# One more down stage in seven block products, one batch's softmax numerators with their sums on ScalarE, and the column-max exchange moved to ScalarE

## The chip, the cores and the metric

The kernel runs on one core of one Trainium2 chip. A core has a matrix engine (PE, with its weight loads PEld), a vector engine (DVE), an activation engine (ACT), a general engine (POOL) and a queue engine for transfers (SP). Each engine takes its instructions strictly in the order of the program and waits at an instruction until the semaphores that it names have been reached. The metric is the device time of one launch in microseconds (us).

## The reference

Eight batches of a linear attention (8 heads, 576 tokens, 64 columns a head) feed one gated feed-forward block over all 4608 tokens:

```python
q_s = np.exp(q - np.max(q, axis=-1, keepdims=True)); q_s = q_s / (np.sum(q_s, axis=-1, keepdims=True) + 1e-09)
k_s = np.exp(k - np.max(k, axis=2, keepdims=True));  k_s = k_s / (np.sum(k_s, axis=2, keepdims=True) + 1e-09)
kv = np.einsum('bhsd,bhse->bhde', k_s, v)
x  = np.einsum('bhsd,bhde->bhse', q_s, kv)           # then (tokens, 512)
h  = (x @ w1) * (x @ w2) @ w3                         # 512 -> 1024 -> 1024
out = h @ w_out                                       # 1024 -> 512
```

q is normalised along a head's 64 columns, k along the 576 tokens. The kernel folds `w3 @ w_out` into one matrix `W3O` (1024 x 512) first.

## The kernel before, in words

**Tiles.** A batch's q, k and v lie in SBUF as 128 partitions: 64 rows of tokens x 2 halves of the heads, each with 4 heads x 9 token slots x 64 columns. The feed-forward works on nine groups of 512 tokens: groups 0 to 7 are the first 512 tokens of a batch each, group 8 gathers the 64 that remain of every batch (`xtail`).

**Steps of a batch b.** `qmx.b.p` (DVE) finds the row maxima of q, `qsub.b.p` (POOL or DVE) subtracts them, `qexp.b.p` (ACT) is the exponential, `qsm.b.p` (DVE) the row sum, `qeps.b.p`, `qrc.b.p` and `qn.b.p` add epsilon, invert and scale, and `qd.b.p` (a transposing transfer on SP's queue) turns the result. p is 0 (token slots 0 to 3, 1024 elements a partition) or 1 (slots 4 to 8, 1280 elements). For k, `kmi.b` (ACT) and `kmx.b` (DVE) find the column maxima within a partition, `cb.b` (eight DVE instructions: transpose, reduce, four small exchanges between neighbouring quarters of the partitions, reduce, transpose) spreads them over the partitions, `ksub.b.hp` subtracts, `kexp.b.hp` (ACT) is the exponential. `vc.b.hp` casts v. `kv.b` multiplies k and v (PE), `kv2.b` scales it, `xm.b` and `xt.b` multiply q with it (PE), and `xs.b`, `xts.b` copy the result x out of PSUM.

**Steps of a group c.** Up stage of groups 0 to 4: `up.1.c` and `up.0.c` (x @ w2, x @ w1; PE, tile `pab`), `bs.c` (copy one to SBUF), `ab.c` (DVE, their product). Up stage of groups 5 to 8: seven products of half-size blocks in place of eight, `um.c.g.1` to `um.c.g.7`, with the sums of blocks `xd`, `ws` before and the copies `ue` and combinations `uc`, `ab` behind. Down stage of groups 0 to 3 and 8: `down.c.t` (four blocks of 128 tokens, eight matmuls of 512 columns each, tile `po`), `os.c.t` copies it out, `st.c.t` stores it. Down stage of groups 4 to 7 (the list `SD`): seven products of half-size blocks, `dm.c.1` to `dm.c.7` (eight matmuls of 256 columns each, tiles `dA`, `dB`, `dC`), with the four block sums `ad.c.1` to `ad.c.4` before, and behind them the copies `de.c.1`, `.7`, `.2`, `.4` and the combinations `dc.c.1` to `dc.c.4`. Products 1, 6, 5 and 3 use one PSUM bank in turn: product 6 may begin only when `de.c.1` has copied product 1 out of it, product 5 only after `de.c.2`, product 3 only after `de.c.4`. The up stage has the same rule for `um.c.g.1`, `.6`, `.5`, `.3` with `ue.c.g.1`, `.2`, `.4`, and for `.7`, `.4` with `ue.c.g.7`.

**What sets the order.** The string `ORDER` lists every step once; a step's instructions are issued to its engine in that order, and a letter behind a slash (A, D, P) says which engine takes a step that several could take. What stands between two steps of different engines in the string has no effect but through PSUM banks and buffers. Steps that use the port that DVE and POOL share are linked, so that they follow each other as listed. PE's list begins with matmuls on zeros that lead nowhere (`zero`).

**The names that the change touches.** `SD` (L242), `FEXP` (L262), `cb` (L441), `qexps` (L537), `down` (L793), `dm` (L890), and `ORDER` (L83). `qexps` exists in the kernel before, and no batch uses it:

```python
for j in range(js.start, js.stop):
    x = hs.start + h
    nc.scalar.activation(out=st["eq", b, p][:, h, j - js.start, :], in_=qb[:, x, j, :],
                         func=AF.Exp, bias=st["qm", b][:, x, j:j + 1],
                         accum_out=st["qr", b][:, x, j:j + 1])
```

Of the kernel before, what the change touches and what calls it, by code (L numbers as in the profile page):

```python
# [93 lines left out]
qsub.1.0/P up.0.0.0.2 kexp.1.1 up.1.0.1.2 qmx.1.1 qsub.1.1/P qexp.1.0 ab.0.1.1 ab.0.0.2 qsm.1.0 qeps.1.0/D qrc.1.0  # L94
qn.1.0/P qd.1.0 kexp.1.0 k.3 up.0.0.0.3 ab.0.0.3 up.0.0.1.2 bs.0.1.2/A ab.0.1.2 qexp.1.1 vc.1.0/A qsm.1.1 qeps.1.1/A
ws.1.1/P ab.0.1.3 q.3 down.0.0 down.0.1 os.0.1/A down.0.2 qrc.1.1 qmx.2.0 kv.1.0 qn.1.1/P qmx.2.1 qsub.2.1/P vc.1.1/A
kv.1 kv2.1 os.0.0/A kmi.2 kmx.2.0 down.0.3 xm.1.0 xs.1.0.0/A xs.1.0.1/D up.1.1.0.0 up.0.1.0.0 kmx.2.1 os.0.2/A cb.2
qexp.2.1 qsm.2.1 bs.1.0.0/A qd.1.1 up.1.1.0.1 up.0.1.0.1 up.1.1.0.2 os.0.3/A bs.1.0.1/A qsub.2.0/P up.0.1.0.2
up.1.1.0.3 up.0.1.0.3 ws.2.1/P xm.1.1 v.2 ab.1.0.0 v.3 ab.1.0.1 xt.1 bs.1.0.2/A ab.1.0.2 qexp.2.0 qsm.2.0 bs.1.0.3/A
ksub.2.1/P ab.1.0.3 down.1.0 down.1.1 qeps.2.1/A qrc.2.1 ksub.2.0/P kmi.3 q.4 kmx.3.0 qeps.2.0/A qrc.2.0 xts.1.1/A  # L100
qmx.3.1 xs.1.1.0/A xs.1.1.1/A os.1.0/A up.1.1.1.0 up.0.1.1.0 up.1.1.1.1 kexp.2.1 qmx.3.0 up.0.1.1.1 qn.2.1/P
up.1.1.1.2 xts.1.0/A vc.2.1/A kmx.3.1 bs.1.1.0/A ab.1.1.0 cb.3 kexp.2.0 qd.2.1 vc.2.0/A bs.1.1.2/A up.0.1.1.2 ab.1.1.2
qn.2.0/P bs.1.1.1/A ab.1.1.1 os.1.1/A qsub.3.1/P qexp.3.1 kv.2 kv2.2 up.1.1.1.3 bs.1.1.3/D up.0.1.1.3 qd.2.0 ab.1.1.3
qsub.3.0/P qexp.3.0 qsm.3.0 ksub.3.0/P xm.2.1 xs.2.1.0/A xm.2.0 xs.2.0.1/A xt.2 xs.2.0.0/A ksub.3.1/P down.1.2 k.4
xs.2.1.1/A up.1.2.0.0 bs.2.0.0/A kexp.3.1 xts.2.1/A qsm.3.1 qeps.3.1/D xts.2.0/A kmi.4 up.0.2.0.0 up.1.2.0.1 st.0.3
up.0.2.0.1 qeps.3.0/A up.1.2.0.2 q.5 kexp.3.0 ws.3.0/D st.0.2 qrc.3.1 wt.1/D ab.2.0.0 bs.2.0.1/A up.0.2.0.2 qmx.4.1
bs.2.0.2/A up.1.2.0.3 vc.3.0/A up.0.2.0.3 qrc.3.0 qn.3.1/P qmx.4.0 up.1.2.0.4 os.1.2/A up.0.2.0.4 up.1.2.0.5 vc.3.1/A
bs.2.0.4/A kmx.4.0 qn.3.0/P ab.2.0.2 kmx.4.1 bs.2.0.5/A qmx.5.1 ab.2.0.1 bs.2.0.3/A ab.2.0.3 v.4 vc.4.1/A qsub.4.0/P
up.0.2.0.5 ab.2.0.4 qsub.4.1/P qexp.4.1 up.1.2.0.6 bs.2.0.6/A kv.3 kv2.3 st.0.1 qd.3.1 ab.2.0.5 qexp.4.0 ws.1.0/P
ws.2.0/D down.1.3 os.1.3/A qd.3.0 xm.3.0 st.0.0 xs.3.0.1/A xm.3.1 xs.3.1.1/A xt.3 xs.3.0.0/A qsub.5.1/P cb.4  # L110
ksub.4.0/P up.0.2.0.6 xts.3.0/A v.5 k.5 qsm.4.1 ab.2.0.6 up.1.2.0.7 xs.3.1.0/A q.6 up.0.2.0.7 up.1.3.0.0 vc.4.0/A v.6
bs.2.0.7/A qsm.4.0 qexp.5.1 bs.3.0.0/A qeps.4.0/A ab.2.0.7 up.0.3.0.0 up.1.3.0.1 up.0.3.0.1 up.1.3.0.2 up.0.3.0.2
st.1.1 qmx.5.0 bs.3.0.1/A ksub.4.1/P ab.3.0.1 qeps.4.1/A qrc.4.1 qrc.4.0 kmi.5 qn.4.0/P ab.3.0.0 up.1.3.0.3 up.0.3.0.3
kexp.4.0 kexp.4.1 k.6 bs.3.0.3/A kmx.5.0 up.1.3.0.4 bs.3.0.4/A qsm.5.1 qsub.5.0/P vc.5.1/A qexp.5.0 kmx.5.1 qeps.5.1/A
xts.3.1/D qn.4.1/P down.2.0 os.2.0/A ab.3.0.3 qmx.6.1 down.2.1 down.2.2 qsub.6.1/P os.2.1/A bs.3.0.2/A qmx.6.0
qsub.6.0/P cb.5 ksub.5.0/P kv.4 kv2.4 up.0.3.0.4 up.1.3.0.5 os.2.2/A qd.4.0 ab.3.0.2 up.0.3.0.5 up.1.3.0.6 up.0.3.0.6
bs.3.0.5/A ab.3.0.5 ksub.5.1/P kmi.6 qexp.6.1 qd.4.1 ab.3.0.4 xm.4.0 st.1.0 qsm.5.0 qrc.5.1 xm.4.1 down.2.3 xs.4.0.1/A
kmx.6.0 qexp.6.0 bs.3.0.6/A xs.4.0.0/D up.1.3.0.7 up.0.3.0.7 ab.3.0.6 xs.4.1.0/A xs.4.1.1/A up.1.4.0.0 up.0.4.0.0
up.1.4.0.1 st.2.2 ws.3.1/D q.7 qeps.5.0/A qrc.5.0 kexp.5.0 kmx.6.1 cb.6 qn.5.0/P qd.5.0 kexp.5.1 bs.4.0.0/A ab.4.0.0
bs.3.0.7/A qn.5.1/P ab.3.0.7 qsm.6.1 vc.6.1/A up.0.4.0.1 os.2.3/A st.2.3 bs.4.0.1/A up.1.4.0.2 up.0.4.0.2 vc.6.0/A  # L120
up.1.4.0.3 up.0.4.0.3 up.1.4.0.4 ab.4.0.1 bs.4.0.2/A ab.4.0.2 qd.5.1 st.1.3 vc.5.0/A qmx.7.0 kv.5 qsm.6.0 ksub.6.0/P
kexp.6.0 xt.4 xts.4.1/A up.0.4.0.4 qeps.6.1/A bs.4.0.4/A ab.4.0.4 kv2.5 bs.4.0.3/A ab.4.0.3 up.1.4.0.5 down.3.0
os.3.0/D st.1.2 up.0.4.0.5 xm.5.0 xm.5.1 ksub.6.1/P kexp.6.1 k.7 qeps.6.0/A qrc.6.0 qsub.7.0/P bs.4.0.5/A ab.4.0.5
wt.3/P qexp.7.0 qsm.7.0 xts.4.0/A kv.6 xs.5.0.1/A xt.5 xs.5.1.1/A xs.5.0.0/A xs.5.1.0/A up.1.4.0.6 qn.6.0/P bs.4.0.6/A
kv2.6 xd.5.3/P um.5.1.1 ue.5.1.1/A qmx.7.1 down.3.1 ws.4.0/D os.3.1/A xd.5.2/D um.5.0.7 ue.5.0.7/A ws.4.1/D xd.5.1/D
um.5.2.1 ue.5.2.1/A xts.5.1/A wt.2/D xts.5.0/A um.5.1.6 ue.5.1.2/A v.7 um.5.0.1 ue.5.0.1/A qeps.7.0/D um.5.1.7
xd.5.4/D kmi.7 wt.4/D down.3.2 qrc.6.1 qsub.7.1/P ue.5.1.7/A qd.6.0 um.5.0.6 um.5.1.4 ue.5.0.2/A kmx.7.0 qrc.7.0
uc.5.1.3 qn.6.1/P qd.6.1 um.5.1.5 ue.5.1.4/A uc.5.1.4/P qexp.7.1 kmx.7.1 um.5.0.4 vc.7.1/A um.5.0.5 uc.5.0.3 st.3.0
ue.5.0.4/A uc.5.0.4/P up.0.4.0.6 ab.4.0.6 um.5.3.1 um.5.2.6 qn.7.0/P up.1.4.0.7 bs.4.0.7/A um.5.2.7 qsm.7.1 um.5.1.3
ue.5.3.1/A cb.7 ksub.7.0/P down.3.3 os.3.2/A um.5.3.7 st.3.1 qeps.7.1/A ue.5.2.7/A um.5.2.4 ab.5.1.1 qrc.7.1 qn.7.1/P  # L130
ue.5.2.2/A uc.5.2.3 um.5.2.5 um.5.3.6 os.3.3/A um.5.1.2 uc.5.1.1 um.5.3.2 uc.5.3.1 um.5.0.3 ab.5.0.1 um.5.2.2 uc.5.2.1
ue.5.3.7/A um.5.3.4 ue.5.3.2/A uc.5.3.3 up.0.4.0.7 ab.4.0.7 vc.7.0/A um.5.3.5 ad.4.3/D ue.5.2.4/A ad.4.1/D um.5.2.3
xm.6.0 xm.6.1 xt.6 ue.5.3.4/A uc.5.3.4/D uc.5.2.4/D qd.7.0 um.5.3.3 xs.6.0.0/A xs.6.1.1/A xs.6.1.0/A dm.4.1 ad.4.2/D
xts.6.0/D dm.4.2 dm.4.7 xs.6.0.1/A um.6.2.1 ad.4.4/D de.4.1/A dm.4.6 xd.6.3/D ksub.7.1/D xts.6.1/D um.5.0.2 uc.5.0.1
kexp.7.0 de.4.7/A dm.4.4 st.3.2 de.4.2/A dm.4.5 dc.4.1 st.2.1 kexp.7.1 ab.5.2.0/P dc.4.3 ue.6.2.1/A um.6.2.7
ue.6.2.7/A de.4.4/A kv.7 qd.7.1 xd.6.2/D xd.6.4/D um.6.2.6 um.6.2.4 ab.5.2.1 dm.4.3 ue.6.2.2/A kv2.7 xd.6.1/P um.6.2.5
dc.4.2/A ab.5.3.0/P ab.5.3.1 ab.5.1.0/P xm.7.1 uc.6.2.3 xm.7.0 xt.7 xts.7.1/D ue.6.2.4/A uc.6.2.4/D xs.7.0.0/A
# [984 lines left out]
```

## Time and profile before

| what | us |
|---|---|
| median of three runs | 228.77 (228.55 to 229.41) |
| the profiled execution, its own time | 228.65 |
| its span, first to last instruction | 226.8 |
| PE busy in the span | 219.9 |
| DVE busy | 202.7 |
| ACT busy | 153.8 |
| POOL busy | 147.9 |

The profiled execution lies 0.12 us under the median, and 1.85 us of its time lie outside the span. In the profile a row of a group gives the line, the engine, the operation, the tiles (written <- read), the shapes, the count, the busy time and the mean length of one. PE's busy time is modelled: neighbouring matmuls overlap in it, so PE's pace is read from the starts of neighbouring groups or from the chain of work that ended last, which gives each piece the time until the next one. On ACT and DVE too an instruction's length is a little more than the distance to the next one.

### The profile page before, as it was taken

The page shows a single profiled execution, that of the slowest core. Times are in us where ns is not written, and L with a number is a line of the kernel's source. Part 1 is how long each engine was busy: PE and PEld are TensorE (multiplying, and loading weights), DVE is VectorE, ACT ScalarE, POOL GpSimd, SP SyncE. Part 2 cuts the span into 40 slices and gives each one's busy share as a digit, 9 for nine tenths or more (in the row PEclk, how much of TensorE's full clock was granted, in tenths as well). Part 3 has the DMA queues.
Part 4 walks back from the last instruction along what each step waited for, and adds up shares of the span by engine and source line. Part 5 has one row for each costly group of instructions (what it writes and reads, how often), then busy time and mean ns, then how long its engine had stood idle before and what let it go on. Part 6 is the DMA issues. An engine that isn't in the chain of part 4 may idle for free.

```text
span 226.8 us, 5607 instructions
## 1 busy us (share of the span) xinstructions
PE 219.9 (97%) x2226; PEld 148.2 (65%) x2226; DVE 202.7 (89%) x381; ACT 153.8 (68%) x250; POOL 147.9 (65%) x100
## 2 busy tenths in 40 slices
...
GB/s 223 212 274 248 298 223 248 372 376 268 342 386 267 286 410 233 264 395 390 168 181 199 152 343 124 98 188 158 3 132 56 0 95 92 3 92 3 95 185 185
DMA packets 38106, 46.89 MB, mean 207 GB/s; under 512 B 18112, under 2 KB 21568, under 8 KB 38080
## 3 DMA queue, kind: packets, MB, share of 16 engines
...
q8 instruction: 17, 0.28, 0.5%
q10 hardware_dynamic: 144, 0.07, 0.1%
q14 instruction: 9, 0.07, 0.1%
...
## 4 chain that ended last, share of the span: by engine, by line
PE 46%; DVE 25%; DMA 18%; ACT 3%; issue 3%; POOL 3%; SPq 1%; DVEq 0%; POOLq 0%
PE uA L858 12%; DMA q<-in_q_dram 7%; PE pab L774 6%; PE dA L899 6%; PE uB L858 6%; DVE ab L789 6%; DVE qm L521 5%; DMA v<-in_v_dram 5%; DMA w<-in_moe_w_dram 5%; DVE qr L553 4%; PE po L796 3%; PE uC L858 3%; PE dB L899 3%; PE po L811 3%; DVE kmp L433 2%
## 5 line engine op out<-in xcount | busy, mean ns | idle before, releaser
L774 PE MATMUL pab<-x,w2sb 128*128 128x256 f16 (+1 forms) x224 | 40.6, 318 | 0.8 <-ACT x L273 0.7
L774 PE MATMUL pab<-x,w1sb 128*128 128x256 f16 (+1 forms) x224 | 40.4, 318 | 0.0
L458 POOL TENSOR_TENSOR k<-k,cb 128x1152 f32<-128x1152 f32 x12 | 31.3, 2625 | 9.0 <-ACT xtail L273 9.0
L527 POOL TENSOR_TENSOR q<-q,qm 128x1024 f32<-128x1024 f32 (+1 forms) x14 | 29.6, 2125 | 6.3 <-DVE aux L1070 3.7
L571 POOL TENSOR_TENSOR en<-eq,qr 128x1024 f16<-128x1024 f16 (+1 forms) x14 | 29.6, 2124 | 4.4 <-ACT xtail L273 2.2
L774 PEld LDWEIGHTS <-w2sb 128*128 128x128 f16 x224 | 21.6, 98 | 14.0 <-issue 1.2
L796 PE MATMUL po<-W3O,ab 128*128 128x512 f16 x128 | 29.7, 380 | 0.2 <-DVE ab L789 0.2
L774 PEld LDWEIGHTS <-w1sb 128*128 128x128 f16 x224 | 21.7, 98 | 11.8
L269 ACT CAST bsb<-pab 128x512 f16<-128x512 f32 x39 | 22.3, 594 | 9.6 <-PE pab L774 9.4
L858 PEld LDWEIGHTS <-w 128*128 128x128 f16 x256 | 24.8, 98 | 4.6 <-DVE v L837 0.3
L789 DVE TENSOR_TENSOR ab<-pab,bsb 128x512 f16<-128x512 f32 x40 | 26.0, 674 | 0.1
L521 DVE TENSOR_REDUCE qm<-q 128x16 f32<-128x1024 f32 (+2 forms) x16 | 21.1, 1333 | 3.1 <-DMA q<-in_q_dram 3.1
L535 ACT ACTIVATE eq<-q 128x1024 f16<-128x1024 f32 (+2 forms) x16 | 18.6, 1170 | 6.0 <-DVE q L527 5.2
L553 DVE TENSOR_REDUCE qr<-eq 128x16 f32<-128x1024 f16 (+2 forms) x16 | 21.3, 1337 | 0.0
L796 PEld LDWEIGHTS <-ab 128*128 128x128 f16 x128 | 12.0, 98 | 14.2 <-DVE ab L789 1.0
L269 ACT COPY v<-uA 128x512 f32<-128x512 f32 x25 | 14.6, 591 | 8.6 <-PE uA L858 7.9
L466 ACT ACTIVATE ek<-k 128x1152 f16<-128x1152 f32 x16 | 18.5, 1172 | 0.9 <-POOL k L458 0.7
L273 ACT ACTIVATE x<-xm 128x512 f16<-128x512 f32 x30 | 16.3, 607 | 3.7 <-PE xm L623 3.6
L858 PE MATMUL uA<-v,w 128*128 128x256 f16 x128 | 18.6, 273 | 0.1
L433 DVE TENSOR_TENSOR kmp<-kmp,k 128x512 f32<-128x512 f32 x21 | 14.5, 690 | 2.7 <-ACT kmp L429 2.4
L269 ACT CAST v<-v 128x1152 f16<-128x1152 f32 x14 | 16.5, 1180 | 0.0
L269 ACT COPY outs<-po 128x512 f32<-128x512 f32 (+1 forms) x18 | 10.4, 581 | 8.7 <-PE po L811 6.9
...
## 6 DMA issues: line engine op xcount, KB each, us to landing
...
```

The source lines that it names most:

```text
L269: return [(nc.scalar.copy if eng == "ACT" else engine[eng].tensor_copy)(out=out, in_=in_)]
L433: top = lambda out, in0, in1: dve.tensor_tensor(out=out, in0=in0, in1=in1, op=ALU.max)
L458: return [engine[eng].tensor_tensor(out=kb[:, two(hp), :, :], in0=kb[:, two(hp), :, :], in1=st["cb", b][:, two(hp), None, :].broadcast_to( ...
L521: dve.tensor_reduce(out=st["qm", b][:, hs, j], in_=qb[:, hs, j, :], axis=AX.X, op=ALU.max, **({"negate": True} if (b, p) in FEXP else {}))
L527: return [engine[eng].tensor_tensor(out=qb[:, hs, j, :], in0=qb[:, hs, j, :], in1=st["qm", b][:, hs, j, None].broadcast_to([P, nh, n, D]), ...
L553: dve.tensor_reduce(out=st["qr", b][(slice(None), *part(p))], in_=st["eq", b, p], axis=AX.X, op=ALU.add)
L571: return [engine[eng].tensor_tensor(out=st["en", b][:, j, hs, :].rearrange("p j h d -> p h j d"), in0=st["eq", b, p], in1=st["qr", b][:, h ...
L774: nc.tensor.matmul(st["p", one, c, sub, u][:, a * (t1 - t0):(a + 1) * (t1 - t0)], lhsT=w[:, ct, fb * P:(fb + 1) * P], rhs=x()[:, ct, t0:t1 ...
L789: dve.tensor_tensor(out=st["ab", c][:, nf * u:nf * u + nf, t0:t1], in0=cut(st["p", 0, c, sub, u]), in1=cut(st["bsb", c, sub, u]), op=ALU.mult)
L796: nc.tensor.matmul(st["po", c, tb], lhsT=st["ab", c][:, ft, tb * P:(tb + 1) * P], rhs=W3O[:, ft, :], start=(ft == 0), stop=(ft == N_FT - 1))
L858: nc.tensor.matmul(t[:, u, :], lhsT=w[:, k0 + kk, fb * P:(fb + 1) * P], rhs=r[:, kk, :], start=(p in (1, 2, 7) and u == 0 and kk == 0), st ...
L899: nc.tensor.matmul(t[:, i, :], lhsT=l[:, f, i * P:(i + 1) * P], rhs=r[:, f, :], start=(p in (1, 2, 7) and i == 0 and f == 0), stop=(i == 1 ...
```

## The change

Four things change.

- Group 3 joins `SD`: its down stage is made of seven products (56 matmuls of 256 columns) with four block sums, four copies and four combinations, in place of 32 matmuls of 512 columns and four copies.
- `FEXP` holds both parts of batch 7: its maxima are taken negated, `qsub.7` and `qsm.7` are gone, and `qexp.7` becomes 36 exponentials of 64 elements a partition with the negated maximum as bias and the row sum as second output. They stand in the list as eight steps, `qexp.7.0.0` to `qexp.7.0.2` and `qexp.7.0` of four each, `qexp.7.1.0` to `qexp.7.1.2` and `qexp.7.1` of five each.
- In batches 3 to 7 the four small exchanges of `cb` are ACT copies (step `cbx`), between the first part (`cbt`) and the last part (`cb`) on DVE.
- `ORDER` is a new list from its 148th step on; 71 of the steps that may run on several engines run on another one than before (`vc.6.0` and `vc.7.0` on POOL, to which no `vc` went before).

```diff
-st.8.3.0 down.8.3 os.8.3.256/D os.8.3/D st.8.3.256 st.8.3
+down.8.3.0 os.8.2/A os.8.3.0/A down.8.3.256 down.8.3 st.8.1 os.8.3.256/D os.8.3/A st.8.2 st.8.3.0 st.8.3.256 st.8.3
...
-    SD = (4, 5, 6, 7)
+    SD = (3, 4, 5, 6, 7)
...
-    FEXP = []
+    FEXP = [(7, 0), (7, 1)]
+    CX = [3, 4, 5, 6, 7]
...
-        def cb():
+        def cb(part=(0, 1, 2)):
+            if 0 in part:
+                cb0()
+            m = st["cbm", b]
+            if 1 in part:
+                for x in range(P // QD):
+                    y = x ^ 1
+                    o, i = m[x * QD:(x + 1) * QD, :, 1], m[y * QD:(y + 1) * QD, :, 0]
+                    if b in CX:
+                        nc.scalar.copy(out=o, in_=i)
+                    else:
+                        dve.tensor_reduce(out=o, in_=i[:, :, None], axis=AX.X, op=ALU.max)
+            if 2 in part:
+                e = work.tile([P, nq], F32, tag="mxe", name="mxe")
+                dve.tensor_reduce(out=e, in_=m, axis=AX.X, op=ALU.max)
+                st["cb", b] = work.tile([P, HH, D], F32, tag="cb", name="cb")
+                dve.transpose(out=st["cb", b].rearrange("p h d -> p (h d)"),
+                              in_=e[:, :, None].broadcast_to([P, nq, QD]))
+
+        def cb0():
             t = work.tile([P, nq, QD], F32, tag="kmq", name="kmq")
...
-            for x in range(P // QD):
-                y = x ^ 1
-                dve.tensor_reduce(out=m[x * QD:(x + 1) * QD, :, 1],
-                                  in_=m[y * QD:(y + 1) * QD, :, 0:1], axis=AX.X, op=ALU.max)
...
-        A(("cb", b), "DVE", cb, [n for n in plan.steps if n[0] == "kmx" and n[1] == b])
+        kmxs = [n for n in plan.steps if n[0] == "kmx" and n[1] == b]
+        if b in CX:
+            A(("cbt", b), "DVE", lambda: cb([0]), kmxs)
+            A(("cbx", b), "ACT", lambda: cb([1]), [("cbt", b)])
+            A(("cb", b), "DVE", lambda: cb([2]), [("cbx", b)], kind="cbe")
+        else:
+            A(("cb", b), "DVE", cb, kmxs)
```

The first place is ACT's list around the exponentials of batch 7. `eq` are the exponentials, `qr` the row sums, `qm` the maxima, `uA`, `uB` products of group 5's up stage that are copied (`ue`), `dA`, `dB` products of group 3's down stage that are copied (`de`), `pab` copied is a `bs` of group 4, `kmp` is `kmi.7`. Before, the second of the two exponentials stands there:

```order
L269 COPY v_1_74<-uA 128x512
L429 COPY kmp<-k_0_69 128x512
L269 COPY v_1_74<-uB 128x512
L269 COPY v_1_74<-uA 128x512 x2
L535 ACTIVATE eq<-q_0_71 128x1280
L269 CAST v_0_75<-v_0_73 128x2x9x64
```

And in the changed kernel, from `de.3.7` to `kmi.7`:

```order
L271 COPY q_1_72<-dB 128x512
L559 ACTIVATE eq,qr<-q_0_71,qm 128x64 x5
L275 ACTIVATE xtail<-xt 128x2x64
L271 COPY q_1_72<-uA 128x512
L559 ACTIVATE eq,qr<-q_0_71,qm 128x64 x4
L271 CAST bsb<-pab 128x512
L559 ACTIVATE eq,qr<-q_0_71,qm 128x64 x18
L271 COPY q_1_72<-dA 128x512
L559 ACTIVATE eq,qr<-q_0_71,qm 128x64 x4
L572 ACTIVATE qr<-qr,epst 128x4x4
L271 COPY q_1_72<-uB 128x512
L431 COPY kmp<-k_0_69 128x512
```

The copy of `dA` is `de.3.1`: 27 exponentials stand between it and `de.3.7`. On PE, `dm.3.6` waits for `de.3.1`; between the end of `dm.3.7` and `dm.3.6` PE's list has `um.5.3.1`, `up.0.4.0.5`, `up.1.4.0.6`, `dm.3.4`, `up.0.4.0.6`, `dm.3.1`, `um.5.3.6`, `dm.3.2` and `um.5.3.7`. Behind `kmi.7` ACT's list goes on with `qeps.7.0`, the last five exponentials and `ue.5.3.2`, for which `um.5.3.5` waits.

The second place is DVE's list around `cb.4`. Before, all eight instructions follow each other:

```order
L443 STREAM_TRANSPOSE kmq<-km 128x256
L446 TENSOR_REDUCE mx<-kmq 128x8
L449 TENSOR_REDUCE mx<-mx 32x8 x4
L452 TENSOR_REDUCE mxe<-mx 128x8
L454 STREAM_TRANSPOSE cb<-mxe 128x256
```

In the changed kernel `kv2.3` and one `ab` of group 2 stand where the exchanges were:

```order
L464 STREAM_TRANSPOSE kmq<-km 128x256
L467 TENSOR_REDUCE mx<-kmq 128x8
L515 TENSOR_SCALAR rc<-pkv 128x2 x2
L516 RECIPROCAL rc<-rc 128x4
L518 TENSOR_TENSOR kv_1492<-pkv,rc 128x2x64 x2
L808 TENSOR_TENSOR ab<-pab,bsb 128x512
L457 TENSOR_REDUCE mxe<-mx 128x8
L459 STREAM_TRANSPOSE cb<-mxe 128x256
```

The four copies now stand in ACT's list, and DVE's `mxe` waits for them.

139 lines of the change are left out of this document (68 added, 71 removed).

## The prediction

> **What bounds the kernel now.** I read first the page's busy times, then the table by stage, then the chain that ended last, then the groups of single stages.
>
> Busy times of the whole span, from the page:
>
> ```profile
> PE 219.9 (97%) x2226; PEld 148.2 (65%) x2226; DVE 202.7 (89%) x381; ACT 153.8 (68%) x250; POOL 147.9 (65%) x100
> ```
>
> By stage (columns: stretch, its length, busy time and count of each engine, granted clock, share of the transfer engines, GB/s):
>
> ```profile
> core 0: us, PE busy (x) PEld busy (x) DVE busy (x) ACT busy (x) POOL busy (x), PEclk, DMA share, GB/s
> 60.00:72.00 12.00, 12.00 (x108) 8.91 (x106) 11.83 (x19) 9.61 (x16) 12.00 (x6) 1.00 1.16 331
> 84.00:96.00 12.00, 12.00 (x138) 5.68 (x136) 11.65 (x27) 11.10 (x18) 10.59 (x6) 1.00 1.00 257
> 128.00:136.00 8.00, 8.00 (x125) 4.35 (x124) 7.86 (x20) 6.78 (x14) 7.21 (x5) 1.00 0.77 261
> 136.00:144.00 8.00, 7.93 (x59) 5.42 (x58) 7.87 (x18) 7.05 (x14) 5.05 (x3) 1.00 0.55 93
> 168.00:216.00 48.00, 48.00 (x443) 42.93 (x441) 43.02 (x72) 22.91 (x43) 23.43 (x19) 1.00 0.25 66
> ```
>
> The clock is 1.00 throughout. From 48 to 144 us PE, DVE, ACT and POOL are all nearly full; behind 168 ACT is idle half the time. The chain gives PE's pace (columns: start, time until the next piece, what, how many instructions):
>
> ```profile
> 145.24 1.73 PE po L796 x8
> ...
> 150.90 0.86 PE pab L774 x4
> ...
> 154.69 0.87 PE dC L899 x8
> ...
> 157.75 0.44 PE uC L858 x4
> ...
> 160.37 0.71 PE pkv L484 x72
> ...
> 163.37 0.56 PE xm L623 x8
> ```
>
> A matmul of 512 columns goes through in 1.73 / 8 = 0.216 us, one of 256 in 0.109. Behind 136 us the chain is PE alone at this pace. Before that PE loses a little. Its groups from 47 to 136 us:
>
> ```profile
> L796 PE MATMUL po<-W3O,ab 128*128 128x512 f16 x112 | 25.9, 380 | 0.2 <-DVE ab L789 0.2
> L774 PE MATMUL pab<-x,w2sb 128*128 128x512 f16 x92 | 23.6, 379 | 0.0
> L774 PE MATMUL pab<-x,w1sb 128*128 128x512 f16 x88 | 22.6, 380 | 0.0
> L774 PE MATMUL pab<-x,w1sb 128*128 128x256 f16 x67 | 8.8, 273 | 0.0
> L774 PE MATMUL pab<-x,w2sb 128*128 128x256 f16 x64 | 8.5, 273 | 0.8 <-ACT x L273 0.7
> L484 PE MATMUL pkv<-v,ek 64*64 64x65 f16 x432 | 4.8, 193 | 0.0
> ```
>
> At the pace above: 292 x 0.216 = 63.1; 131 x 0.109 = 14.3; 432 / 72 x 0.71 = 4.3; the products with q I put at 4.2 (four groups like the `xm` of 0.56, the narrower ones not over 2); 11 matmuls of `um` 1.2. Together 87.1 of 89: PE loses about 1.9 us here, waiting for DVE and ACT, of which one wait shows (0.7, ACT's copy of x).
>
> **The change, part by part.** Durations for the added and removed instructions:
>
> ```profile
> L535 ACT ACTIVATE eq<-q 128x1024 f16<-128x1024 f32 (+2 forms) x16 | 18.6, 1170 | 6.0 <-DVE q L527 5.2 <-POOL q L527 0.4
> L553 DVE TENSOR_REDUCE qr<-eq 128x16 f32<-128x1024 f16 (+2 forms) x16 | 21.3, 1337 | 0.0
> L269 ACT CAST v<-v 128x1152 f16<-128x1152 f32 x14 | 16.5, 1180 | 0.0
> L269 ACT CAST bsb<-pab 128x512 f16<-128x512 f32 x39 | 22.3, 594 | 9.6 <-PE pab L774 9.4
> L837 DVE TENSOR_TENSOR k<-ab 128x1024 f16<-128x1024 f16 x8 | 5.3, 685 | 0.1
> L837 POOL TENSOR_TENSOR k<-ab,k 128x1024 f16<-128x1024 f16 x2 | 4.2, 2122 | 9.0 <-DVE k L837 5.8 <-PE uA L858 3.2
> L449 DVE TENSOR_REDUCE mx<-mx 32x8 f32<-32x8 f32 x32 | 4.9, 153 | 0.6
> L458 POOL TENSOR_TENSOR k<-k,cb 128x1152 f32<-128x1152 f32 x12 | 31.3, 2625 | 9.0 <-ACT xtail L273 9.0
> ```
>
> *Group 3 in seven products.* PE: 32 x 0.216 = 6.9 go, 56 x 0.109 = 6.1 come: 0.8 less, on the path. DVE gains three block sums and two combinations of 0.69 and loses one copy: +2.7; POOL one sum of 2.1 and one combination; ACT four copies and `dc.3.2` for three `os`: +1.0. Two stores of twice the size replace four on SP, which has nothing urgent behind them. What is new on the path is that a product must wait for ACT's copy of the one before it in its bank.
>
> *The exchanges on ACT.* 20 x 0.15 = 3.1 us leave DVE. On ACT the nearest row is a scaling of 128 elements (below), 0.16 apart: 20 x 0.16 = 3.2, bounds 2 and 6. DVE now waits for ACT inside `cb`; queued behind that wait are `ab` steps, for which PE waits. Cover: `kv2.3` and an `ab` for `cb.4`, 1.5 us, in other batches two to three steps, against four small copies and the copy or cast of 0.6 to 1.2 ahead of them on ACT. I take zero; without the cover it costs up to 1 us in each of four batches.
>
> *`qsub.7` and `qsm.7` gone.* DVE loses 2 x 1.34 = 2.7. POOL loses two subtractions like the ones of `k`, and gets two casts of v: one input of 1152 elements, between ACT's 1.2 and the 2.6 of POOL's subtraction; I take 2.3. POOL ends about even, and hides it except ahead of `dm.3.7`, where `ksub.6` (twice 2.6) and `ad.3.3` (2.1) follow `cb.6` in a row; zero, up to 1 us.
>
> *The new order.* Until PE turns to group 5 (about 133 us), DVE sheds 16 exchanges (2.4), the copies `os.3.0`, `bs.1.1.3` and two `xs` (2.7) and `qsm.7.0` (1.3), and takes up group 3's sums, one combination and one difference of weights (3.5): about 3 us less. Of PE's 1.9 lost there I take 1.4 as regained; bounds 0 and 1.9. So far: 228.65 - 0.8 - 1.4 = 226.4.
>
> *The 36 exponentials.* No row shows an exponential of 64 elements, a bias that differs by row in an exponential, or a sum as second output. The nearest rows on ACT (start, length, what):
>
> ```profile
> 126.78 0.26 ACT L273 ACTIVATE xtail<-xt 128x128 f16<-128x128 f32 x1
> 126.94 0.30 ACT L559 ACTIVATE qr<-qr,epst 128x20 f32<-128x20 f32 x1
> 127.14 1.06 ACT L269 CAST bsb<-pab 128x512 f16<-128x512 f32 x2
> ...
> 136.00 0.59 ACT L269 COPY q<-uB 128x512 f32<-128x512 f32 x1
> 136.47 0.60 ACT L269 COPY q<-uA 128x512 f32<-128x512 f32 x1
> ```
>
> An element costs (1180 - 594) / 640 = 0.9 ns. Without a bias 128 elements took 0.16 to the next instruction, so 64 would take 0.10. With a bias from memory 20 elements took 0.20, so 64 take 0.24. The sum can cost nothing, or at most one more instruction of that kind, 0.20. Ends: 0.10 and 0.44. I take 0.24, the row with a bias, and for the sum a little under half of 0.20: 0.33. Then 36 x 0.33 = 11.9 us replace two of 1.2 on ACT, +9.5.
>
> Where they stand decides. Between `dm.3.7` and `dm.3.6` PE has three `um` pieces (3 x 0.44), three `up` (3 x 0.86) and three `dm` (3 x 0.87): 6.5 us. ACT has in that time `de.3.7`, `ue.5.3.1` and `bs.4.0.6` (0.48 each, the distance of two copies), `xts.5.1` (0.16), 27 exponentials, and `de.3.1` (0.58 until its end): 2.2 + 27 x 0.33 = 11.1. `dm.3.6` waits for `de.3.1`: PE stands still for 11.1 - 6.5 = 4.6 us. Then ACT needs four exponentials, `qeps.6.0`, `ue.5.3.7`, `kmi.7`, `qeps.7.0`, five exponentials and `ue.5.3.2`: 1.9 + 9 x 0.33 = 4.9, while PE has `dm.3.6`, `up.1.4.0.7` and three `um` until `um.5.3.5`: 0.87 + 0.86 + 1.31 = 3.0. Another 1.8. Sum 6.4. Queued behind on ACT are copies of group 5 that PE reaches later: `de.3.2` costs 0.1 more, then ACT has caught up. In these 10 us DVE would have cost PE a few tenths, which now hide under the stall: -0.4. So +6.1 on the path, and behind 150 us nothing gives it back, since PE has no slack there. 226.4 + 6.1 = **232.5 us**.
>
> At an end of 0.24 the two stalls are 2.2 and 1.0, with -0.3: 229.3. At 0.44, 7.6 and 2.8: 236.6. At 0.16 or less both are gone.
>
> The Trainium skill bears on this price (ScalarE: Activation LUTs, "What ACT_TABLE_LOAD costs"): it states about 280 ns + 0.833 ns an element for an ACTIVATE with a bias from memory, with 93 ns overlapped by the next one, which is 0.24 for 64 elements if the sum is free. By that page the sum would be 229.3, by my middle 232.5; the row of 0.20 agrees with the page on the bias, and no run here shows the sum.
>
> **Rivals.**
>
> *The sum is free* (0.24 each). For it: the bias alone explains every row there is. Against: a second output has to be written somehow, and nothing here shows that for nothing. Time 229.3, 228.8 to 230.2.
>
> *The burst is covered and the kernel is faster.* The exponentials cost 0.16 or less, as the scaling without a bias does, and the list is tight without a stall. For it: with 0.14 both waits come out just met, as tightly as waits elsewhere in the order. Against: the row with a bias. It decides from 27 exponentials under 4.3 us on. Time 226.4, from 225.9 (all of PE's loss regained) to 227.8 (only the 0.8).
>
> *Another engine takes over:* DVE waits inside `cb`, or POOL's row ahead of `dm.3.7` is late, on top of the burst. For it: POOL's 12.00 of 12 at 60 us, ACT's 11.10 at 84. Against: two to three us of other work between the parts of `cb`. With 2 to 4 us it gives 234 to 237 beside the burst, 229 to 231 without it.
>
> *The seven products bring nothing:* a gain of 0.8 us is all there is, so even without it the result moves by 0.3%.
>
> **How the numbers follow.** Half a per cent, 1.1 us, is what a measurement of this kernel tells from no change: slower is above 229.9, faster below 227.6. The burst at more than 0.25 each, with or without another wait: 0.62, slower. The sum free: 0.15, half of it inside half a per cent. Covered: 0.14 faster, 0.02 same. Another engine alone: 0.07, three in seven inside half a per cent. Slower 0.73, same 0.13, faster 0.14. The likeliest case by itself spans 229.9 to 236.6. The range of 8 in 10 goes from 227.6 to 237.0: below it lies the covered case, above it the whole price of a second instruction with another wait.
>
> **What would show it.** Right: the 36 exponentials 0.28 to 0.40 apart between about 126 and 142 us, PE idle before a `dA` matmul for 3 to 6 us and before a `uA` matmul for 1 to 2, both released by ACT, ACT full in that stretch; the last `um` of group 8 about 4 us later than before. Wrong: exponentials 0.15 apart or less and no such idle time; PE losing more than 2 us before 125 us; DVE waiting for ACT's `mx`.

## The result and the profile after

The changed kernel takes 236.47 us (median; 236.21 to 236.78), the kernel before 228.67 us on the same chip: a ratio of 1.0335 (95%: 1.0309 to 1.036). It is 7.8 us slower, where 3.8 were forecast. The profiled execution took 236.21 us, its span 234.4.

Busy times of the whole span, from the page of the changed kernel:

```profile
PE 221.2 (94%) x2250; PEld 151.7 (65%) x2250; DVE 198.1 (85%) x358; ACT 170.1 (73%) x349; POOL 144.1 (61%) x98
```

By stage, changed kernel (columns as in the table before: stretch, length, busy time and count of PE, PEld, DVE, ACT and POOL, granted clock, transfer share, GB/s):

```profile
48.00:60.00 12.00, 10.69 (x138) 6.19 (x136) 11.58 (x27) 9.51 (x14) 11.65 (x6) 1.00 1.06 264
60.00:128.00 68.00, 67.82 (x689) 36.44 (x688) 65.35 (x120) 62.81 (x111) 64.47 (x30) 1.00 1.06 298
128.00:136.00 8.00, 8.00 (x136) 5.57 (x135) 7.65 (x16) 7.92 (x31) 1.22 (x2) 1.00 0.80 283
136.00:144.00 8.00, 3.05 (x22) 2.31 (x21) 2.02 (x4) 8.00 (x47) 3.22 (x2) 0.91 0.26 57
144.00:150.00 6.00, 6.00 (x39) 3.71 (x38) 5.68 (x16) 6.00 (x20) 3.83 (x3) 0.84 0.23 44
150.00:160.00 10.00, 10.00 (x96) 8.40 (x94) 9.52 (x19) 9.61 (x22) 4.85 (x5) 1.00 0.52 135
```

PE loses its time in one place, from 136 to 144 us, where it was busy 7.93 of 8 us before and is busy 3.05 now. ACT is full there, and DVE and POOL are busy for 2.0 and 3.2 of the 8 us. From 144 to 150 us PE counts as busy all the time, but at a granted clock of 0.84. The chain that ended last runs over ACT from 128.6 us to the start of `dm.3.6` at 142.35, and from 75 us to the last matmul it leaves PE nowhere else. Its end there:

```profile
135.88 5.95 ACT eq L559 x36
141.83 0.48 ACT q L271
...
142.35 1.72 PE dA L918 x8
144.07 1.71 PE pab L793 x4
```

The exponentials hold the chain (18 of them in this piece, two instructions each), then the copy `de.3.1` (L271), then `dm.3.6` and `up.1.4.0.7`. The last two take 1.72 and 1.71 us, where eight matmuls of 256 columns took 0.87 and four of 512 took 0.86 before. ACT's own instructions (start, length):

```profile
131.63 0.41 ACT L559 ACTIVATE eq<-q,qm 128x64 f16<-128x64 f32 x1
131.88 0.25 ACT L559 ACTIVATION_READ_ACCUMULATOR eq<-q,qm 128x1 f32 x1
131.98 0.39 ACT L559 ACTIVATE eq<-q,qm 128x64 f16<-128x64 f32 x1
```

and their groups, with the group of the exchanges:

```profile
L559 ACT ACTIVATE eq<-q,qm 128x64 f16<-128x64 f32 x36 | 12.2, 377 | 0.0
L559 ACT ACTIVATION_READ_ACCUMULATOR eq<-q,qm 128x1 f32 x36 | 8.3, 230 | 0.0
L452 ACT COPY mx<-mx 32x8 f32<-32x8 f32 x20 | 3.9, 196 | 1.3 <-DVE mx L467 1.1
```

Each call makes two instructions on ACT: the exponential, and one that reads the sum out. They overlap, and the two together come 0.33 us apart over the whole burst. PE in the same place, and its longest wait:

```profile
142.35 1.72 PE L918 MATMUL dA<-aux,k 128*128 128x256 f16 x8 [4.95 <-ACT q L271]
...
147.22 0.61 PE L877 MATMUL uA<-v,w 128*128 128x256 f16 x4
```

The first row is `dm.3.6`, the second `um.5.3.5`. The end of the run differs as well. Landing times of the two last stores (x1, size, us from issue to landing) in the changed kernel:

```profile
out_dram<-outs SPq DMA_DIRECT2D x1, 64.0 KB, 2.7
out_dram<-outs ACTq DMA_DIRECT2D x1, 64.0 KB, 2.5
```

and one of them in the kernel before:

```profile
out_dram<-outs ACTq DMA_DIRECT2D x1, 64.0 KB, 1.6
```

In the changed kernel the last matmul ends 6.4 us later than before (230.35 against 223.98), and from there to the end of the span it is 4.05 us instead of 2.8. A transfer of 8 KB of instructions (queue 14) runs there at 231.42 us, for 0.91 us; before, the last such transfer ran at 209.0.

### The profile page after: what moved, and what is told of

The parts are those of the page before. It is cut to its first block, busy times and chain, and to the rows that moved or that the text cites. A ratio compares the mean times of both kernels' runs of the same rounds, so it can differ in the third digit from the quotient of the medians.

```text
span 234.4 us, 5717 instructions
## 1 busy us (share of the span) xinstructions
PE 221.2 (94%) x2250; PEld 151.7 (65%) x2250; DVE 198.1 (85%) x358; ACT 170.1 (73%) x349; POOL 144.1 (61%) x98
## 4 chain that ended last, share of the span: by engine, by line
PE 61%; DMA 19%; POOL 6%; ACT 6%; DVE 5%; issue 2%; POOLq 0%
PE pab L793 18%; PE uA L877 12%; PE dA L918 7%; DMA q<-in_q_dram 7%; PE uB L877 6%; DMA v<-in_v_dram 5%; DMA w<-in_moe_w_dram 5%; PE po L815 4%; ACT eq L559 4%; PE uC L877 3%; PE dB L918 3%; PE po L830 3%; DMA qT<-en 2%; POOL k L471 2%; DVE qm L534 2%
## 5 line engine op out<-in xcount | busy, mean ns | idle before, releaser
L793 PE MATMUL pab<-x,w2sb 128*128 128x256 f16 (+1 forms) x224 | 41.5, 323 | 0.9 <-ACT x L275 0.9
L271 ACT CAST bsb<-pab 128x512 f16<-128x512 f32 x40 | 23.1, 596 | 4.7 <-PE pab L793 4.6
L540 POOL TENSOR_TENSOR q<-q,qm 128x1024 f32<-128x1024 f32 (+1 forms) x12 | 25.4, 2127 | 0.2 <-DVE qm L534 0.2
L815 PE MATMUL po<-W3O,ab 128*128 128x512 f16 x96 | 22.4, 379 | 0.0
L548 ACT ACTIVATE eq<-q 128x1024 f16<-128x1024 f32 (+2 forms) x14 | 16.4, 1168 | 6.3 <-DVE q L540 5.8
L918 PEld LDWEIGHTS <-k 128*128 128x128 f16 x160 | 15.8, 99 | 7.2 <-issue 5.1
L275 ACT ACTIVATE x<-xm 128x512 f16<-128x512 f32 x31 | 16.9, 618 | 4.5 <-PE xm L636 4.5
L271 ACT COPY v<-uA 128x512 f32<-128x512 f32 x25 | 14.9, 600 | 6.8 <-PE uA L877 5.2
L566 DVE TENSOR_REDUCE qr<-eq 128x16 f32<-128x1024 f16 (+2 forms) x14 | 18.7, 1339 | 0.0
L271 ACT COPY q<-uA 128x512 f32<-128x512 f32 x21 | 12.1, 605 | 6.8 <-PE uA L877 2.8
L815 PEld LDWEIGHTS <-ab 128*128 128x128 f16 x96 | 9.1, 98 | 10.3
```

Of the source, the lines that this page charges most:

```text
L271: return [(nc.scalar.copy if eng == "ACT" else engine[eng].tensor_copy)(out=out, in_=in_)]
L540: return [engine[eng].tensor_tensor(out=qb[:, hs, j, :], in0=qb[:, hs, j, :], in1=st["qm", b][:, hs, j, None].broadcast_to([P, nh, n, D]), ...
L566: dve.tensor_reduce(out=st["qr", b][(slice(None), *part(p))], in_=st["eq", b, p], axis=AX.X, op=ALU.add)
L793: nc.tensor.matmul(st["p", one, c, sub, u][:, a * (t1 - t0):(a + 1) * (t1 - t0)], lhsT=w[:, ct, fb * P:(fb + 1) * P], rhs=x()[:, ct, t0:t1 ...
L815: nc.tensor.matmul(st["po", c, tb], lhsT=st["ab", c][:, ft, tb * P:(tb + 1) * P], rhs=W3O[:, ft, :], start=(ft == 0), stop=(ft == N_FT - 1))
L918: nc.tensor.matmul(t[:, i, :], lhsT=l[:, f, i * P:(i + 1) * P], rhs=r[:, f, :], start=(p in (1, 2, 7) and i == 0 and f == 0), stop=(i == 1 ...
```

## The experiments

Theory A in the expectations is the prediction's mechanism with the sizes just read: ACT's list around the exponentials makes PE wait. The rivals are told with each run. Ratios are to the kernel before, with 95% intervals.

### What an exponential costs, and what the stall hides

**e1: the sums left out.** The row sums are set to one, so the exponentials have no second output.

```diff
+                    dve.memset(st["qr", b], 1.0)
...
-                                     func=AF.Exp, bias=st["qm", b][:, x, j:j + 1],
-                                     accum_out=st["qr", b][:, x, j:j + 1])
+                                     func=AF.Exp, bias=st["qm", b][:, x, j:j + 1])
```

> The changed kernel with the row sums of batch 7 left out (the 36 exponentials have no second output, the sums are set to 1 by one DVE memset). Theory A: the sum is a second ACT instruction of 0.09 us each, ACT's list up to the copy ue.5.3.2 sets when PE goes on, and the slow matmuls behind the stall are hidden under that. Then the exponentials stand 0.24 apart, PE's idle time ahead of dm.3.6 falls from 5.0 to about 2.5, um.5.3.5 starts 36 x 0.09 = 3.2 us earlier, and the time is 233.2 (232.7 to 233.7). Theory B: idle time and slow matmuls add up on PE's path, so both fall: 5.0 to 2.5, and most of the 1.8 of slow matmuls goes: about 232.2 or less. If the sum were free: 236.4, no change.

231.74 us, ratio 1.0126 (1.0106 to 1.0147). The total is what theory B gave, but 1.0 us of it comes from the end of the run, of which neither theory knew; without it the time would be 232.7, the lower end of theory A's range. The exponentials now start 0.238 us apart, so the sum costs 0.093 us each, 3.3 us for 36. PE in this run, `dm.3.6`, `up.1.4.0.7` and `um.5.3.5`:

```profile
139.50 1.03 PE L918 MATMUL dA<-aux,k 128*128 128x256 f16 x8 [2.49 <-ACT q L271]
140.37 1.03 PE L793 MATMUL pab<-x,w2sb 128*128 128x512 f16 x4
...
143.53 0.61 PE L877 MATMUL uA<-v,w 128*128 128x256 f16 x4 [0.48 <-ACT v L271]
```

The wait is halved (2.49 for 4.95) and the matmuls behind it keep their pace. `um.5.3.5` starts 3.7 us earlier, and the last matmul ends 4.0 us earlier; the further 1.0 us is the end of the run, where the load of instructions no longer falls among the last stores (e6). From `dm.3.6` to `um.5.3.5` it is now 4.03 us in place of 4.87: that is 9 x 0.093 less, the nine exponentials that ACT has in between, as theory A has it. The Trainium skill (ScalarE: Activation LUTs, "What ACT_TABLE_LOAD costs") gives 280 ns + 0.833 ns an element with a bias from memory, 93 ns of it overlapped: an estimate of 0.24 for 64 elements. This run's 0.238 agrees.

After 2.49 us of idle time no matmul was slow; after 4.95 us they took up to twice as long, and the granted clock was 0.51 from 142.5 to 146.0 us. The Trainium skill (TensorE: Matmul & The Clock Gate, "What's actually happening") speaks of half rate after an idle window of about 3.4 us, until PE has been busy for as long; these two runs agree with it. The length of a single wait doesn't decide it, as e3, e4 and e7 show (last section).

**e2: the copy ahead of the burst.** `de.3.1` moves from behind `dm.3.2` to right behind `dm.3.1`, ahead of 18 exponentials (the expectation says 22).

```diff
-... bs.4.0.6/A dm.3.1 ws.4.0/D qexp.7.0.1 ... ab.4.0.5 dm.3.2 de.3.1/A dc.3.1 ...
+... bs.4.0.6/A dm.3.1 de.3.1/A ws.4.0/D qexp.7.0.1 ... ab.4.0.5 dm.3.2 dc.3.1 ...
```

> The changed kernel with one step moved: de.3.1 stands right behind dm.3.1, ahead of 22 of the 27 exponentials on ACT that it stood behind. Theory A (ACT's whole list up to ue.5.3.2 sets the end, and that list is as long as before): dm.3.6 runs without a wait, PE stands still ahead of um.5.3.4 and um.5.3.5 instead, um.5.3.5 starts at 147.2 as in the changed kernel, and the time is 236.4 within 0.5; up to 1.5 more if the matmuls are slow behind the later stall, where nothing hides it. Theory B (the wait of dm.3.6 for de.3.1 is the price, the copies behind it have room): 5 us less, 231.4.

236.89 us, ratio 1.0352 (1.0321 to 1.0383). `dm.3.6` no longer waits, and nothing is gained. PE, then DVE:

```profile
144.26 1.01 PE L877 MATMUL uC<-x,w1sb 128*128 128x256 f16 x4 [5.66 <-DVE kv L518]
...
146.78 1.06 PE L877 MATMUL uA<-v,w 128*128 128x256 f16 x4
```

```profile
143.34 0.25 DVE L577 RECIPROCAL qr<-qr 128x16 f32<-128x16 f32 x1 [6.07 <-ACT qr L572]
```

PE stops two pieces later, before `um.5.3.2`. It waits for `kv2.6` on DVE, which is queued behind `qrc.6.0`, which waits for `qeps.6.0`, which ACT issues behind the burst. `um.5.3.5` starts at 146.78 instead of 147.22 us. The wait belongs to the burst and not to the one copy; whatever of ACT's results PE needs first takes it over.

**e3: PE kept busy.** 44 matmuls of zeros are added into the bank of `um.5.3.7`, so that PE isn't idle ahead of `dm.3.6`.

```diff
+    WARM = 44
...
+                    for _ in range(WARM if (c, g, p, u, kk) == (5, 3, 7, 1, 1) else 0):
+                        nc.tensor.matmul(t[:, u, :], lhsT=zero[:, 0:P], rhs=zero[:, 0:256],
+                                         start=False, stop=False, ...)
```

> The changed kernel with 44 matmuls on zeros of 256 columns (4.8 us at PE's pace) inside um.5.3.7, which add nothing to its sum and fill most of PE's idle time ahead of dm.3.6. If the idle time is what makes the matmuls behind it slow, dm.3.6, up.1.4.0.7 and um.5.3.2 run in 0.87, 0.86 and 0.44 instead of 1.51, 1.71 and 0.63. Theory A: um.5.3.5 then waits for ue.5.3.2 for 1.5 to 1.8 us more and starts at 147.1 as before: the time is 236.4 within 0.4. Theory B: the slow matmuls cost their 1.8 us on the path: 234.7.

237.3 us, ratio 1.0352 (1.0296 to 1.0407), so nothing is gained. PE in this run:

```profile
138.81 4.97 PE L879 MATMUL uB<-zero 128*128 128x256 f16 x44
144.04 1.03 PE L922 MATMUL dA<-aux,k 128*128 128x256 f16 x8 [0.16 <-ACT q L272]
144.91 1.03 PE L794 MATMUL pab<-x,w2sb 128*128 128x512 f16 x4
146.49 0.60 PE L881 MATMUL uC<-x,w1sb 128*128 128x256 f16 x4 [0.55 <-DVE kv L519]
...
148.92 0.61 PE L881 MATMUL uA<-v,w 128*128 128x256 f16 x4 [0.95 <-POOL v L272]
```

`dm.3.6` and `up.1.4.0.7` are back at full pace, yet `um.5.3.5` again starts 4.88 us behind `dm.3.6` (147.22 - 142.35 = 4.87 in the changed kernel): two waits stand where the slow matmuls were. The second is put down to POOL; the copy `ue.5.3.2` on ACT, which PE needs as well, ended 0.06 us before PE went on. So the slow matmuls cost nothing in the changed kernel, since ACT's list set the time behind `dm.3.6` too. The totals say less: the four runs lie between 235.57 and 238.3 us, and in the profiled one PE falls 2.0 us behind the changed kernel in another place, from 53 to 62 us (last section).

### The same order with other softmax steps

**e5: the burst taken away.** The 36 exponentials become one plain exponential a part, with no maximum subtracted and no sum taken (the sums are set to one).

```diff
-            for j in range(js.start, js.stop):
-                x = hs.start + h
-                nc.scalar.activation(...)
+                    dve.memset(st["qr", b], 1.0)
+            if h == nh - 1:
+                nc.scalar.activation(out=st["eq", b, p], in_=qb[:, hs, js, :], func=AF.Exp)
```

> The changed kernel with the 36 exponentials replaced by one plain exponential for each part of batch 7, at the places of the last ones of each part (the maximum isn't subtracted and the row sums are set to 1: two DVE memsets of 36 elements; nothing else is left out). It leaves the order, the seven products and the exchanges on ACT, and takes ACT's 11.9 us down to 2.4. Theory A: the burst cost PE all of 5.1 + 1.8 us, and the loss of 3.8 us that PE has before 127 us is as large in the new order as in the old: the last matmul ends about 7 us earlier, and the time is 229.0 (228.4 to 229.8), no better than the kernel before. Rival, the base of the prediction: without the burst the new order is worth what I took, 226.4 to 227.6.

228.01 us, ratio 0.9963 (0.995 to 0.9977). By stage, and PE behind `um.5.3.7`:

```profile
136.00:144.00 8.00, 8.00 (x66) 6.16 (x64) 7.61 (x20) 7.70 (x14) 7.85 (x6) 1.00 0.47 90
```

```profile
137.08 1.04 PE L916 MATMUL dA<-aux,k 128*128 128x256 f16 x8
137.95 1.03 PE L791 MATMUL pab<-x,w2sb 128*128 128x512 f16 x4
```

There is no wait and no slow matmul. All that the change does apart from the burst is thus worth -0.85 us (95%: -0.5 to -1.1), which is what the seven products were to give (-0.8), with batch 7's subtraction and sums gone from POOL and DVE besides. The changed kernel is 8.5 us slower than this run; in the profiles 7.2 us of that stand at the end of the last matmul (230.35 against 223.13), and 1.0 comes from the end of the run.

**e4: two exponentials in the new order.** `FEXP` is empty; the subtractions stand behind `xd.5.1` on POOL, the exponentials behind `de.3.2` and `de.3.4`, the sums on DVE.

```diff
-    FEXP = [(7, 0), (7, 1)]
+    FEXP = []
...
+... xd.5.1/P qsub.7.0/P qsub.7.1/P ... de.3.2/A qexp.7.0 ... de.3.4/A qexp.7.1 ... um.5.2.1 qsm.7.0 ...
```

> The changed kernel without the 36 exponentials: batch 7 has qsub.7 (POOL, behind xd.5.1), two exponentials (ACT, behind de.3.2 and de.3.4) and qsm.7 (DVE) again; the rest of the order, the seven products of group 3 and the exchanges on ACT stay. Theory A: the exponentials cost all of PE's stall, 5.1 + 1.8 us, and the order costs nothing beside them: 229.6, down to 229.0 if the last stores land as early as in the kernel before. Rival: the work that comes back to DVE and POOL (2.7 and 4.2 us) makes PE wait in 140 to 165 us: 230.5 to 232. A third: the order is better than the old one without the burst: under 227.6.

234.27 us, ratio 1.0233 (1.0211 to 1.0255): the rival is right that the work that comes back makes PE wait, and its 230.5 to 232 was too low. PE's waits:

```profile
PE uA L877 <- ACT v L271: 2.3, 1, 2.3
PE uB L877 <- DVE ab L856: 1.2, 1, 1.2
PE uB L877 <- ACT v L271: 0.9, 1, 0.9
```

and by stage:

```profile
144.00:150.00 6.00, 3.42 (x29) 2.62 (x27) 4.42 (x6) 1.08 (x3) 6.00 (x6) 1.00 0.54 100
```

ACT was busy for 1.08 of 6 us: it stood for 4.28 us in `qeps.7.1`, which needs the row sum `qsm.7.1` that DVE began at 148.57, with copies that PE needed queued behind it. Ahead of that sum in DVE's list stood a combination that waited 1.21 us for POOL. Behind the waits the granted clock was 0.50 from 153.2 to 156.6 us.

**e9: the same, placed later.** As e4, but the softmax steps of batches 6 and 7 and some 15 neighbours are placed so that no engine should meet a result that isn't ready (`um.5.3.7` earlier, `qexp.7.1` and `qsm.7.1` later).

```diff
+... bs.4.0.6/A um.5.3.7 dm.3.1 ... qsub.7.0/P qeps.6.0/A qsub.7.1/P ... de.3.2/A qexp.7.0 ... uc.5.3.3 qsm.7.0 ... um.5.3.3 qexp.7.1 ... uc.5.2.1 qsm.7.1 ...
```

> The changed kernel with two plain exponentials for batch 7 in place of the 36, as in the run with two exponentials, but with the steps of the softmax of batches 6 and 7 and some fifteen neighbours moved so that ACT never stands behind a wait for POOL or DVE: qsub.7 behind qrc.6.1, qexp.7.0 behind de.3.2, qexp.7.1 some ten steps later, qsm.7 later still. Theory A: what is left of the price is the work of qsub.7 and qsm.7 (4.2 us on POOL, 2.7 on DVE), which costs PE 1 to 3 us between 140 and 157 us: 229.8 (229.0 to 231.0), between the run without any exponentials (228.0) and the one where they stood badly (234.3). Rival: the new order has no room for that work at all, wherever it stands: 232 or more. A third: with the steps placed well the seven products' 0.8 us remain: under 228.4.

232.94 us, ratio 1.0175 (1.0113 to 1.0237). That is better than e4 by 1.3 us and far from the 228 of e5; it lies in the rival's range. PE's longest wait in the middle is now

```profile
PE xm L636 <- ACT x L275: 1.6, 1, 1.6
```

and the last stores land in 2.6 to 2.7 us again, about 1 us of the total (e6). Two attempts don't show that no order with two exponentials is as fast as the old one; none was found.

### The exponentials in the old order

**e10.** The kernel before with the 36 exponentials alone, in eight groups between ACT's steps at the old places; the seven products stay at groups 4 to 7, the exchanges on DVE, and the rest of the order as before.

```diff
-    FEXP = []
+    FEXP = [(7, 0), (7, 1)]
+    CX = []
...
-... wt.3/P qexp.7.0 qsm.7.0 xts.4.0/A kv.6 xs.5.0.1/A xt.5 ...
+... wt.3/P qexp.7.0.0 xts.4.0/A kv.6 xs.5.0.1/A qexp.7.0.1 xt.5 ...
```

> The kernel before with one part of the change alone: the 36 exponentials of batch 7 (no qsub.7, no qsm.7), in eight groups with two to three of ACT's other steps between them, at the places of the two exponentials; order, exchanges on DVE and the four 512-column down stages of group 3 are those of the kernel before. ACT gets 36 x 0.331 - 2.4 = 9.5 us more between about 128 and 155 us, where it is idle for some 4 us; DVE sheds 2.7, POOL 4.2. Theory A: ACT's list has no room there in this order either, PE waits for ue copies by about 5 to 7 us: 234.5 (233.5 to 236.5). Rival: it is the new order that puts the exponentials ahead of the copies, and in groups between the old steps they are hidden: 228.2 to 229.5.

238.07 us, ratio 1.0394 (1.0372 to 1.0416): theory A's way, and above its range. PE:

```profile
154.33 1.01 PE L877 MATMUL uB<-v,w2sb 128*128 128x256 f16 x4 [3.43 <-ACT v L271]
155.14 1.91 PE L877 MATMUL uA<-v,w 128*128 128x256 f16 x8
156.84 1.48 PE L877 MATMUL uC<-x,w1sb 128*128 128x256 f16 x6
```

and by stage:

```profile
150.00:160.00 10.00, 6.27 (x31) 4.31 (x31) 2.89 (x6) 7.84 (x25) 6.92 (x4) 0.66 0.59 96
```

The 36 exponentials alone cost 9.0 us in the old order (238.07 / 1.0394 = 229.05), more than the whole change does in the new one. Spread out they give four waits of PE for ACT, DVE and POOL (3.4, 1.2, 0.9, 0.7 us) and here the slow matmuls come on top: eight in 1.70 us (155.14 to 156.84) that need 0.87. So the new order isn't what makes the exponentials dear; ACT had no room for them around 130 to 160 us in either of the two lists.

### The exchanges, DVE's load and the end

**e7: the exchanges alone.** The kernel before, with `cbt` and `cbx` right behind `kmx` in batches 3 to 7 and `cb` two or more DVE steps later.

```diff
-... kmx.3.1 bs.1.1.0/A ab.1.1.0 cb.3 kexp.2.0 ...
+... kmx.3.1 cbt.3 cbx.3 bs.1.1.0/A ab.1.1.0 kexp.2.0 ... ab.1.1.2 cb.3 ...
```

> The kernel before with one part of the change alone: the exchanges of cb on ACT in batches 3 to 7, cbt placed right behind kmx and cb two or more DVE steps later; SD, the exponentials and the rest of the order are those of the kernel before. It takes 20 x 0.15 = 3.1 us from DVE and gives ACT 20 x 0.2 = 4 us. Theory A: PE's loss up to 127 us consists of changes of shape and of a chain of transfers and copies at 53 to 58 us, and DVE's load has no part in it: 228.7 within 0.6. Rival, a term of the prediction: a DVE that is 3 us lighter gives PE back 1.4 us: 227.3. A third: DVE's wait for ACT inside cb costs up to 1 us a batch: 230 to 232.

238.56 us, ratio 1.0421 (1.0392 to 1.0449). None of the theories gave this. Waits of all engines:

```profile
ACT mx L452 <- DVE mx L467: 9.1, 5, 3.1
...
PE pkv L497 <- ACT v L271: 4.2, 2, 2.7
PE pab L793 <- ACT bsb L271: 1.9, 1, 1.9
```

I had looked at DVE waiting for ACT's copies. It is ACT that waits, for `cbt` on DVE, 9.1 us in five places, with the casts and copies that PE needs queued behind. Behind the longest wait of PE the granted clock was 0.50 from 76.4 to 79.8 us. In the changed kernel the same 20 copies waited 1.1 us in all (the group above), with other steps between `cbt` and `cbx`. There no wait of PE names them, and here the move costs 9.6 us (238.56 / 1.0421 = 228.9). The two lists differ in more than these places, so that the place alone makes the difference is argued and not tried. What the exchanges gave back on DVE this run couldn't show.

**e8: no exchanges at all.** The kernel before without the four exchanges of every batch (each maximum is then that of a quarter of the rows), which takes 4.9 us off DVE and puts nothing elsewhere.

```diff
-            for x in range(P // QD):
-                y = x ^ 1
-                dve.tensor_reduce(out=m[x * QD:(x + 1) * QD, :, 1], ...)
...
+            dve.tensor_reduce(out=e, in_=m[:, :, 0:1], axis=AX.X, op=ALU.max)
```

> The kernel before without the four small exchanges of cb in all eight batches (the column maxima of neighbouring quarters of the partitions are not combined; nothing takes the place of the exchanges on any engine). DVE is 8 x 4 x 0.153 = 4.9 us lighter, 3.7 of it before 127 us, and ACT no heavier. Theory A: PE's loss of 3.7 us up to 127 us is made of changes of shape and of the chain at 53 to 58 us, DVE's load has no part in it: 228.4 (227.9 to 228.9). Rival, a term of the prediction: PE gains back 1.4 us from a DVE that is three us lighter: 227.3 or less.

228.22 us, ratio 0.9981 (0.995 to 1.0012): between 1.1 us faster and 0.3 slower, so the rival's 1.4 lies outside. By stage, the kernel before and then this run:

```profile
60.00:128.00 68.00, 67.87 (x687) 36.05 (x685) 66.34 (x130) 58.37 (x93) 61.92 (x28) 1.00 1.01 285
```

```profile
60.00:128.00 68.00, 68.00 (x688) 36.28 (x687) 64.80 (x117) 58.92 (x94) 63.13 (x29) 1.00 0.98 288
```

Summing, matmul by matmul, what the distance to the next one exceeds PE's pace from 40 to about 128 us, PE lost 3.7 us before, 3.8 in the changed kernel and 3.1 here. So about 0.6 us of it went with DVE's load, in one trace of each. In the kernel before PE idles 0.13 us from 60 to 128 by the table, and 0.97 us from 48 to 60 (busy 11.03 of 12). The rest of the 3.7 is pauses too short to show as idle, most of them where one kind of matmul follows another, and a DVE that was 3.7 us lighter left them nearly as they were.

**e6: the end.** Two more `memset` on DVE at the very start of the changed kernel, nothing else. Theory T is that the load of instructions among the last stores costs the last microsecond.

```diff
-    dve.memset(ones, 1.0)
+    for _ in range(3):
+        dve.memset(ones, 1.0)
```

> The changed kernel with two more DVE memsets of one element a partition at the very start, so that each later DVE instruction stands two places further in the program. In the changed kernel's trace a load of 8 KB of instructions falls among the last stores (231.4 us, 0.91 us long) and the last store lands 2.5 us after its issue instead of 1.6; in the runs without sums and with two exponentials, which have one and two more DVE instructions, that load stands 1 to 1.5 us ahead of the last matmul. Theory T: the load sits on a count of DVE's instructions, two more move it ahead of the stores, the last store lands after 1.6 us, and the time falls by about 1.0, to 235.4. Rival: the order of the last copies and stores is what takes longer, 236.4, no change.

235.52 us (234.54 to 235.73), ratio 1.0275 (1.0249 to 1.0301). The two last stores in this run:

```profile
out_dram<-outs SPq DMA_DIRECT2D x1, 64.0 KB, 1.6
out_dram<-outs ACTq DMA_DIRECT2D x1, 64.0 KB, 1.6
```

The 8 KB load runs at 228.17 us here, ahead of the last stores, and they land 1.6 us after their issue, as before. From the end of the last matmul to the end of the span it is 3.2 us instead of 4.05. The medians differ by 0.95 us; the ratios, each to the kernel before as measured beside it, by 1.4, with an uncertainty of 0.8. Theory T holds.

The other traces fit it. DVE's rows in the trace (semaphores included) number 450 in the changed kernel, e2, e3 and e9: there such a load runs 1.0 to 1.3 us behind the last matmul, and the last two stores land in 2.4 to 2.7 us. They number 451 or 452 in e1, e4, e5 and e6: there it runs 1.4 to 1.5 us ahead of that end, and the stores land in 1.6. Not every load at the end delays them: in e8 one runs 1.5 us behind the last matmul, and the stores land in 1.6.

## Why the prediction was right and wrong

The sign and the mechanism were right; the size was half of what came (+3.8 for +7.8). Four terms of the sum make up the miss: 1.4 and 0.4 us that were never regained, 1.2 us at the end of the run, and 0.5 us of the stall. Its steps in turn:

- **The price of an exponential, 0.33: right.** Measured 0.331 (0.238 and 0.093 for the sum). The rival of a free sum is out: e1 shows what it would have given, and the sum is not free.
- **The stall before `dm.3.6`, 4.6 us: nearly right.** From the start of `de.3.7` to the end of `de.3.1` ACT took 11.13 us (11.1 forecast), PE's work took 6.6 (6.5). The stall came out 0.5 larger (5.0 to 5.1 us) because ACT began `de.3.7` late, behind four copies of x; the step treated both engines as starting level.
- **The second 1.8 us: right in size, other in form.** `um.5.3.5` starts 4.87 us behind `dm.3.6` (4.9 forecast). The time shows as slow matmuls and not as a wait; e3, where it is waits, gives the same distance.
- **"Of PE's 1.9 lost there I take 1.4 as regained": wrong, 1.4 us.** The 1.9 was a difference of 87.1 and 89, of sums in which the products with q were put at a guess. A table of the stages from 48 to 144 us shows 0.97 us of PE's idle time before 60 us and 0.20 behind it; e8 shows that DVE's load had little to do with what PE lost (0.6 us for a DVE that is 3.7 lighter), and e5 that everything beside the burst gives 0.85 us and not 0.8 + 1.4 = 2.2. The bound of 0 that was given was the right value.
- **"Now hide under the stall: -0.4": wrong, 0.4 us.** Nothing was there to be hidden; this falls with the step above.
- **The end of the run: missing from the sum, 1.2 us.** The load of instructions that now falls among the last stores. e6 shows 0.9 of it (4.05 us behind the last matmul against 3.2); the profile before held no such case, but the sum took the time behind the last matmul as fixed without saying so.
- **The exchanges at zero: right in this order** (ACT waited 1.1 us in all, and no wait of PE names them), though with a danger that was not seen: in e7 it is ACT that waits, 9.1 us, and not DVE. **POOL at about even: right**, 144.1 us for 147.9 (a cast of v took 1.15 us where 2.3 were taken), and no wait of PE for it ahead of `dm.3.7`. **The seven products at -0.8: consistent** with e5, which can't separate them from the other parts.

From 232.5 the sum of the misses goes 1.4 + 0.4 + 0.5 + 1.2 = 3.5, to 236.0; the 0.2 us that remain to 236.2, the profiled time, were not traced. The rival "another engine" gave 234 to 237 and so the measured time, but for a reason that the trace doesn't show: DVE waited, 5.1 us in `dc.3.1` for ACT, inside the stall and not in its place.

What stays open: the losses of PE between 48 and 60 us (1.3 us idle of 12 in the changed kernel, 1.0 before) belong to a chain of transfer of q, product with q, copy of x and up stage; that this is the cause was read from the profile and not tried.
